# The first product of three token blocks as seven half-size products (Strassen), with its weight sums in the staging and attention memory

## The chip, the cores and the metric

The kernel runs on one core of a Trainium2 chip. A core has five engines that run side by side and meet only through semaphores: TensorE (PE in the profile; its weight loads are shown apart as PEld), VectorE (DVE), ScalarE (ACT), GpSimd (POOL) and SyncE (SP), which here issues nearly all DMAs. PE multiplies a stationary 128x128 tile with a moving tile of up to 512 columns and writes to PSUM, of which there are eight banks. The metric is the device time of one execution in microseconds, the median of several.

## The reference, cut to what matters

```python
kv = einsum('bhsd,bhse->bhde', k, v)                 # attention without softmax
o = einsum('bhsd,bhde->bhse', q, kv)
x = (o / sqrt(mean(o * o) + 1e-6) * g_norm)          # -> 2304 tokens x 512
h = x @ w_in                                         # first mixture: 512 -> 2048
g = h * tanh(softplus(h))
y = g @ w_out                                        # 2048 -> 512
h2 = y @ w2_in                                       # second mixture: 512 -> 1024
e = exp(h2 - max(h2)); s = h2 * e / sum(e)
ln = (s - mean(s)) / sqrt(var(s) + 1e-6) * g_ln
out = ln @ w2_out                                    # 1024 -> 512
```

Everything is in float32. The kernel holds each float32 operand of a product as two float16 halves, high and low, and makes three of the four products (high x high, high x low, low x high); so every product on PE costs three matmuls per 128 rows of contraction.

## The kernel before

The 2304 tokens are six blocks of 384 (`NB`, `BLK`). The first mixture goes by units (block, group): a group is four of the sixteen 128-wide slices of `w_in`'s output, so there are 24 units. A unit's first product is the task `H`: `h_mm` (line 636) makes, for each of four slices f, 12 matmuls of 128x384 (four slices of contraction, three passes) into one of three PSUM banks (`psH`, line of matmuls `hp<-xT,w`). ACT applies the activation straight from PSUM (`mish`, line 646, tile `m`), then writes the high half of g (`g_hi`, line 653), and DVE the low half (`g_lo`, line 658); three g buffers (`NG`) and three m buffers (`NM`) turn over. The second product is the task `Y`: `y_mm` (line 676), 48 matmuls of 128x384 per unit into four banks. Blocks 0 to 2 go in two halves of groups; blocks 3 to 5 (the late blocks) go through all four groups in turn, and their result is split to high and low by `y_hi` and `y_lo` (lines 704, 712).

Weights come as float32 pieces of 128x512 words: 16 of `w_in`, 16 of `w_out`, 8 of `w2_in`, 8 of `w2_out`, in the order of `PIECES`. Each is loaded into one of five staging slots (`st`), passes ACT, POOL and DVE to get an exact float32 (`w_scale`, `w_sign`, `w_low`, `w_put`, lines 542 to 559; tile `P`, five buffers), and is then split (`w_hi`, `w_lo`, lines 570, 577). The pieces of `w2_out` also get the factor `g_ln` (line 593) and the sums that a Strassen product needs (`w4_sums`, line 600), then their halves (lines 611, 615). Before the change `w2_in` has a tile of its own (`w3`) in memory that attention leaves when the last transposed x is there (`open_w34`), and `w2_out`'s sums are laid over `w_in`'s memory (`w4`), slice by slice as the last unit's products leave it.

The second mixture goes by 18 tiles of 128 tokens: `emit_H2` (line 753, 24 matmuls of 128x512), then a chain of maximum (DVE, line 764), exponential (ACT, 770), product with the sum (DVE, 779), variance (ACT, 786), norm (DVE, 814), and its split and transposing DMAs (lines 830, 836, 842). H2 of tile t waits for line 779 of tile t-2, which frees its PSUM banks. The output product of two tiles together, task `O` (`emit_O`, line 861), is already made as seven half-size products of 12 matmuls of 128x256, with the orders of `PROD` and `ORDER`, and combined through `o_keep`, `o_add` and `o_copy`.

The order of every engine's instructions is written by a planner. Every piece of work is a task with an engine, an estimated cost, its predecessors and sometimes a due time; `Plan.order` runs a list schedule over estimated times, and `Plan.search` repeats it 300 times with due times of early tasks moved at random and keeps the order whose estimated last PE task ends first. Each engine then gets its instructions in that order and works through them strictly in turn. Where the planned time of a PE task lies more than half a microsecond after the one before it, and before 150 us, `keep_warm` puts in matmuls on the identity (line 1200, 128x256) whose result nobody reads; here they are called fillers. They are executed whether or not the wait they stand for comes.

Of the kernel before, what the change touches and what calls it, by code (L numbers as in the profile page):

```python
# [36 lines left out]
class Plan:  # L37
    def __init__(self):
        self.tasks = {}
        self.behind = {}  # L40

# [68 lines left out]
    def search(self, turns, spread):  # L110
# [9 lines left out]
        for at, k in best:  # L120
            if self.tasks[k][5] is not None:
                self.tasks[k][5] = at
# [18 lines left out]
def tile_attn_moe_moe2(  # L141
# [57 lines left out]
    dec_p = ctx.enter_context(pool("dec", NDEC, side="right"))  # L199
# [19 lines left out]
    units += [(b, g) for b in range(NI, NB) for g in range(4)]  # L219
    line = ["H", "H", "H"]  # L220
# [11 lines left out]
    for u in pe:  # L232
        nominal[u] = at_
        at_ += 48 * MM if u[0] in "HY" else 24 * 0.216 if u[0] == "2" else 84 * 0.1095
# [244 lines left out]
    def a_xT(b, r):  # L479
        t = xhl_t.pop((b, r))  # L480
        if r == 0:
            if b == 2:
# [26 lines left out]
    def w3_item(j):  # L509
# [6 lines left out]
        return load, (lambda: (w34["w3"][:, c, 0, s], w34["w3"][:, c, 1, s])), None, 1  # L516
# [10 lines left out]
    PIECES += [("3", j) for j in range(8)] + [("4", j + o) for j in range(4) for o in (0, 4)]  # L527
# [3 lines left out]

    def w_load(u):
        t = st_all[:, PIECES.index(u) % NST]
        items[u][0](t)
        piece[u] = [t, None]

    def w_scale(u):

        piece[u][1] = dec_p.tile([128, 512], FP32, tag="P", name="P")
# [33 lines left out]
    def w_lo(u):  # L573
# [4 lines left out]
        else:  # L578
# [63 lines left out]

    def mish(b, grp, i):
# [6 lines left out]
    def g_hi(b, grp, i):  # L650
        if i == 0:
# [67 lines left out]
    def open_w34():  # L719
# [3 lines left out]
        w34["w3"] = p.tile([128, C, 2, F2], FP16, name="w3")  # L723
# [14 lines left out]
    T = {}  # L738

# [4 lines left out]
    def emit_H2(t):  # L744
        hp = ph2[t % 2].tile([128, 2, 512], FP32, tag="h2", name="h2")
        w3 = w34["w3"]
# [21 lines left out]
    def s_exp(t):  # L768
        e = T[t, "e"] = ph2["p"].tile([128, F2], FP32, tag="e", name="e", bufs=1)
# [83 lines left out]
    def emit_O(p, i):  # L853
# [5 lines left out]
        for kk in range(4):  # L859
            for la, wa in PASS:  # L860
                nc.tensor.matmul(  # L861
                    out=T[p, bank][:, 0:HB], lhsT=lnTs[p % 2][:, 8 * x + 4 * la + kk],
                    rhs=w4[:, kk, wa, w], start=(first and m == 0),
# [10 lines left out]
    def osb(p, t):  # L874
        if (p, "osb", t) not in T:
            T[p, "osb", t] = dec_p.tile([128, DM], FP32, tag="P", name="osb")
# [27 lines left out]
    load_after = {}  # L904

    for n, u in enumerate(PIECES):
        opened = ("open",) if u[0] in "34" else None
        if n < NST:
            before = []
        else:  # L910
            before = [("put", PIECES[n - NST])]
# [359 lines left out]
```

## Time and profile before

| | |
|---|---|
| median of 3 runs | 617.48 us (616.27 to 617.89) |
| the profiled execution | 616.5 us, its span 614.5 us |
| PE busy | 602.5 us (98%) |
| DVE, ACT, POOL busy | 365.0, 289.5, 95.9 us |
| granted TensorE clock | 1.0 in every slice (the upper level, 2.4 GHz) |
| HBM | 72 GB/s over the span |

The span runs from the first to the last instruction; the profiled time has 2.0 us around it. PE is busy from slice 1 to slice 40 with hardly a gap, so a time of this kernel is a sum over what PE has to issue, plus the few places where it waits. The other engines have idle time in every stage, but unevenly: DVE is at two to five tenths in the middle of the span and at eight to nine tenths in the first tenth and in most of the last third.

### The profile page before, as it was taken

The page shows a single profiled execution, that of the slowest core. Times are in us where ns is not written, and L with a number is a line of the kernel's source. Part 1 is how long each engine was busy: PE and PEld are TensorE (multiplying, and loading weights), DVE is VectorE, ACT ScalarE, POOL GpSimd, SP SyncE. Part 2 cuts the span into 40 slices and gives each one's busy share as a digit, 9 for nine tenths or more (in the row PEclk, how much of TensorE's full clock was granted, in tenths as well). Part 3 has the DMA queues.
Part 4 walks back from the last instruction along what each step waited for, and adds up shares of the span by engine and source line. Part 5 has one row for each costly group of instructions (what it writes and reads, how often), then busy time and mean ns, then how long its engine had stood idle before and what let it go on. Part 6 is the DMA issues. An engine that isn't in the chain of part 4 may idle for free.

```text
span 614.5 us, 10823 instructions
## 1 busy us (share of the span) xinstructions
PE 602.5 (98%) x4427; PEld 382.7 (62%) x4427; DVE 365.0 (59%) x626; ACT 289.5 (47%) x498; POOL 95.9 (16%) x126
## 2 busy tenths in 40 slices
PE   7998999999999999999999999999999999999997
PEld 6676666666666665666666656664445756675586
DVE  1788788882023541334212258995978678878881
ACT  3668557663323423333333266763545535454551
POOL 1534532310000210012101133210011000000000
PEclk9999999999999999999999999999999999999999
DMA  8999675842022250005100175300230993657466
GB/s 290 323 267 223 176 165 172 264 102 73 1 78 71 59 129 1 0 18 77 28 1 2 24 259 197 104 0 2 50 71 1 178 226 95 138 102 149 92 144 149
DMA packets 125904, 69.11 MB, mean 112 GB/s; under 512 B 100000, under 2 KB 117408, under 8 KB 125856
## 3 DMA queue, kind: packets, MB, share of 16 engines
q1 hardware_dynamic: 125696, 68.44, 45.7%
q8 instruction: 34, 0.56, 0.4%
q14 instruction: 14, 0.11, 0.1%
q10 hardware_dynamic: 160, 0.00, 0.0%
HBM read 39.33 MB, written 4.72 MB: 72 GB/s over the span
## 4 chain that ended last, share of the span: by engine, by line
PE 90%; DMA 6%; ACT 2%; issue 1%; DVE 1%; POOL 0%; SPq 0%; POOLq 0%; ACTq 0%
PE y L676 31%; PE hp L636 29%; PE h L753 15%; PE op L861 12%; DMA st<-in_moe_w_in_dram 3%; PE kvp L297 2%; PE xo L435 1%; DMA w<-g 1%; DMA qraw<-in_q_dram 1%; DMA xT<-xhl 1%; DMA yT<-in_k_dram 1%; ACT P L542 0%; POOL rho L457 0%; PE rT L373 0%; ACT m L646 0%
## 5 line engine op out<-in xcount | busy, mean ns | idle before, releaser
L676 PE MATMUL y<-g,w 128*128 128x384 f16 x1152 | 201.2, 326 | 0.0
L636 PE MATMUL hp<-xT,w 128*128 128x384 f16 x960 | 166.0, 326 | 0.6 <-DMA xT<-xhl 0.6
L636 PEld LDWEIGHTS <-w 128*128 128x128 f16 x1152 | 111.9, 98 | 74.3 <-issue 1.2
L676 PEld LDWEIGHTS <-w 128*128 128x128 f16 x1152 | 111.8, 98 | 73.9
L658 DVE SCALAR_TENSOR_TENSOR g<-m,g 128x768 f16<-128x768 f32 x48 | 46.2, 963 | 85.8 <-ACT g L653 85.8
L646 ACT ACTIVATE m<-hp 128x384 f32<-128x384 f32 x96 | 46.3, 488 | 107.6 <-PE hp L636 106.9
L753 PE MATMUL h<-w,yT 128*128 128x512 f16 x432 | 96.0, 379 | 0.0
L861 PE MATMUL op<-w,w 128*128 128x256 f16 x756 | 85.2, 273 | 1.8 <-DMA w<-g 1.0
L861 PEld LDWEIGHTS <-w 128*128 128x128 f16 x756 | 73.8, 98 | 13.5 <-DMA w<-g 1.3
L753 PEld LDWEIGHTS <-yT 128*128 128x128 f16 x432 | 42.3, 98 | 48.0
L547 POOL TENSOR_SCALAR st<-st 128x512 f32<-128x512 f32 x48 | 42.9, 903 | 110.6 <-ACT P L542 110.6
L653 ACT ACTIVATE g<-m 128x768 f16<-128x768 f32 x48 | 40.2, 839 | 13.2 <-PE y L676 12.6
L552 DVE SCALAR_TENSOR_TENSOR st<-st 128x512 int32<-128x512 int32 x48 | 35.9, 759 | 12.0 <-POOL st L547 12.0
L542 ACT ACTIVATE P<-st 128x512 f32<-128x512 f32 x48 | 32.0, 673 | 19.3 <-DMA st<-in_moe_w_in_dram 12.2
L455 POOL TENSOR_SCALAR ms<-ms 128x8 f32<-128x8 f32 x15 | 5.4, 363 | 210.5 <-DVE ms L450 210.1
L559 DVE SCALAR_TENSOR_TENSOR P<-P,st 128x512 int32<-128x512 int32 x48 | 34.9, 748 | 0.1
L636 PE MATMUL hp<-yT,w 128*128 128x384 f16 x192 | 33.3, 326 | 0.0
L805 POOL TENSOR_SCALAR var<-var 128x1 f32<-128x1 f32 x18 | 4.3, 241 | 168.4 <-DVE var L800 168.4
L786 ACT ACTIVATE e<-Q,nmz 128x1024 f32<-128x1024 f32 x18 | 20.7, 1148 | 20.6 <-DVE nmz L782 20.5
L764 DVE TENSOR_REDUCE mx<-h 128x1 f32<-128x1024 f32 x18 | 22.0, 1221 | 11.9 <-PE h L753 11.9
L770 ACT ACTIVATE e<-h,nb 128x1024 f32<-128x1024 f32 x18 | 20.0, 1110 | 15.7 <-DVE nb L765 8.5
L779 DVE SCALAR_TENSOR_TENSOR Q<-h,e 128x1024 f32<-128x1024 f32 x18 | 21.9, 1219 | 6.5 <-ACT e L770 6.5
(105 smaller groups left out, 518.5 us busy)
## 6 DMA issues: line engine op xcount, KB each, us to landing
st<-in_moe_w_in_dram SPq DMA_DIRECT2D x24, 512.0 KB, 5.7
st<-in_moe_w_out_dram SPq DMA_DIRECT2D x24, 512.0 KB, 4.1
yT<-in_k_dram SPq DMA_DIRECT2D x16, 288.0 KB, 5.3
yT<-in_v_dram SPq DMA_DIRECT2D x16, 288.0 KB, 5.6
out_dram<-osb SPq DMA_DIRECT2D x18, 256.0 KB, 2.8
qraw<-in_q_dram SPq DMA_DIRECT2D x3, 768.0 KB, 6.1
qraw<-in_q_dram SPq DMA_DIRECT2D x4, 384.0 KB, 8.3
qraw<-in_q_dram SPq DMA_DIRECT2D x4, 192.0 KB, 5.0
```

The costliest lines, as they stand in the source:

```text
L542: nc.scalar.activation(out=P, in_=v[:, :, 1], func=ACTF.Copy, scale=2.0 ** -111)
L547: nc.gpsimd.tensor_scalar(out=v[:, :, 1], in0=v[:, :, 1], scalar1=0.0, scalar2=1.0, op0=ALU.mult, op1=ALU.mult)
L552: nc.vector.scalar_tensor_tensor(out=v[:, :, 0], in0=v[:, :, 0], scalar=29, in1=v[:, :, 1], op0=ALU.logical_shift_right, op1=ALU.bitwise_or)
L559: nc.vector.scalar_tensor_tensor(out=P.bitcast(I32), in0=P.bitcast(I32), scalar=3, in1=v[:, :, 0], op0=ALU.logical_shift_left, op1=ALU.bit ...
L636: nc.tensor.matmul(out=h_t[b, grp, i], lhsT=w1[:, f, c, wa], rhs=xT_t[b][:, C * xa + c], start=(c == 0 and m == 0), stop=(c == C - 1 and m ...
L646: nc.scalar.activation(out=m_t[b, grp, i // 2][:, i % 2], in_=h_t.pop((b, grp, i)), func=ACTF.Mish, scale=2.0 ** -16)
L653: nc.scalar.activation(out=g_t[b, grp][:, 0, 2 * i:2 * i + 2], in_=m_t[b, grp, i], func=ACTF.Copy, scale=64.0)
L658: nc.vector.scalar_tensor_tensor(out=g_t[b, grp][:, 1, j], in0=m_t.pop((b, grp, i)), scalar=64.0, in1=g_t[b, grp][:, 0, j], op0=ALU.mult, ...
L676: nc.tensor.matmul(out=y_t[cc][:, 0:BLK], lhsT=w2[:, grp * G + ii, wa, cc * 128:(cc + 1) * 128], rhs=g_t[b, grp][:, ga, ii], start=(first ...
L753: nc.tensor.matmul(out=hp[:, half], lhsT=y[:, c, ya, tok], rhs=w3[:, c, wa, half * 512:(half + 1) * 512], start=(m == 0), stop=(m == 3 * C ...
L764: nc.vector.reduce_max(out=mx, in_=T[t, "hp"], axis=AX.X)
L861: nc.tensor.matmul(out=T[p, bank][:, 0:HB], lhsT=lnTs[p % 2][:, 8 * x + 4 * la + kk], rhs=w4[:, kk, wa, w], start=(first and m == 0), stop ...
```

## The change

The first product of blocks 3 to 5 is made as a 2x2 by 2x2 block product in seven block products. The unit (512 contraction rows x 512 outputs x 384 tokens) is cut in half in each of the three; a block product `h_prod` is 12 matmuls of 128x192 (two output slices, two slices of contraction, three passes). Per unit these are 84 matmuls of 128x192 where there were 48 of 128x384. Three of the products use the plain weights and three the plain x, the others sums of them:

- `conv_w` makes the four sums of a group's weights from its halves, in float32 on DVE, and splits the sums again (ACT and DVE): once for each of four groups. `conv_x` does the same for x of each late block. They go one after the other through one scratch `W_` of 2048 words, which is staging slots 2 and 3.
- The sums `ws` lie in staging slots 0 and 1 (group 0), in the `P` buffers (group 1), and in a tile that is opened where attention lay (groups 2 and 3). The sums of x lie in `yT[3]`, `yT[4]` and one more `xT` buffer.
- The seven products go into the three `psH` banks in the order 1, 2, 6, 7, 5, 4, 3; products 6, 5, 4 and 3 add on top of a bank after it was copied out: `h_keep` (ACT) copies a bank, `h_add` (DVE) adds a bank to a copy, `h_act` (ACT) applies the activation, twice from memory and once from PSUM.

What had its place there moves: `w2_in`'s halves are now laid over `w_in` groups 0 and 1, so their last two steps wait for the last block's products of these groups; the pieces of both `w2` matrices pass four staging slots and four `P` buffers, the first two slots being free only after the last block's group 0, the other two after the last sums; `w2_out`'s sums lie in four places and are made in the order 2, 3, 0, 1; the exponential's output shares memory with the scratch of `w4_sums`, so the first exponential waits for the last split of `w2_out`. The transposes of x for the late blocks get fixed due times (190, 222 and 246 us). Since the tasks changed, the planner's search ends in another order everywhere, the first 60 us included.

```diff
 PIECES += [("1", f) for f in range(8, 16)] + [("2", f) for f in range(8, 16)]
-    PIECES += [("3", j) for j in range(8)] + [("4", j + o) for j in range(4) for o in (0, 4)]
+    PIECES += [("3", j) for j in range(8)] + [("4", j + o) for j in (2, 3, 0, 1) for o in (0, 4)]
...
+    w3 = w1f[:, 0:2 * C * F2].rearrange("p (c a n) -> p c a n", c=C, a=2)
...
+    ws = {0: st_w[:, 0:2048].bitcast(FP16), 1: dec_w[:, 0:4096]}
...
+    W_ = st_w[:, 2048:4096].bitcast(FP32)
+    he = st_w[:, 4096:5120].bitcast(FP32)
...
+    def conv_w(g, step):
+        V = W_.rearrange("p (f c n) -> p f c n", f=G, c=C)
+        if step < 2:
+            f = slice(G * g + 2 * step, G * g + 2 * step + 2)
+            nc.vector.tensor_tensor(
+                out=V[:, 2 * step:2 * step + 2].rearrange("p f c n -> p (f c) n"),
+                in0=w1[:, f, :, 0].rearrange("p f c n -> p (f c) n"),
+                in1=w1[:, f, :, 1].rearrange("p f c n -> p (f c) n"), op=ALU.add)
+        elif step < 6:
+            o, x, y, op = c_sums(w_view(V))[step - 2]
+            nc.vector.tensor_tensor(out=o, in0=x, in1=y, op=op)
+        else:
...
+            if not lo:
+                nc.scalar.activation(out=d[:, 0, s], in_=W_[:, s], func=ACTF.Copy)
+            else:
+                nc.vector.tensor_tensor(
+                    out=d[:, 1, s], in0=W_[:, s], in1=d[:, 0, s], op=ALU.subtract)
...
+    HPROD = {1: (0, 0, 0, 0, 0, 0, "A", True), 2: (0, 0, 1, 0, 1, 0, "B", True),
+             6: (1, 0, 0, 1, 1, 1, "A", False), 7: (1, 1, 0, 1, 0, 1, "D", True),
+             5: (1, 1, 1, 1, 0, 0, "A", False), 4: (0, 1, 1, 1, 1, 0, "D", False),
+             3: (1, 0, 1, 0, 1, 1, "A", False)}
...
+    def h_prod(b, grp, i):
+        ww, m, k, xx, kx, n, bank, opens = HPROD[i]
+        p = h_bank(b, grp, bank)
+        S = ws[grp].rearrange("p (a f c n) -> p a f c n", a=2, f=G, c=C)
+        x = xs[b] if xx else xT_t[b]
+        for fs in range(2):
+            f = 2 * m + fs
+            for c in range(2):
+                for j, (wa, xa) in enumerate(PASS):
+                    lhsT = S[:, wa, f, 2 * k + c] if ww else w1[:, G * grp + f, 2 * k + c, wa]
+                    nc.tensor.matmul(
+                        out=p[:, HT * fs:HT * fs + HT], lhsT=lhsT,
+                        rhs=x[:, C * xa + 2 * kx + c, HT * n:HT * n + HT],
...
+    def h_keep(b, grp, n):
+        p = h_bank(b, grp, {1: "A", 2: "A", 7: "D"}[n])
+        nc.scalar.activation(out=h_e(b, grp, n), in_=p[:, 0:BLK], func=ACTF.Copy)
...
+    def h_add(b, grp, m, n, bank, e):
+        p = h_bank(b, grp, bank)
+        nc.vector.tensor_tensor(
+            out=h_m(b, grp, m)[:, :, HT * n:HT * n + HT],
+            in0=p[:, 0:BLK].rearrange("p (f t) -> p f t", f=2),
+            in1=h_e(b, grp, e).rearrange("p (f t) -> p f t", f=2), op=ALU.add)
...
+        elif n < 36:
+            before = [("put", v) for v in PIECES[27:32]]
+            before += [("H", NB - 1, 0, 0)] if n < 34 else [("cx", NB - 1, 9), ("cw", 3, 9)]
         else:
-            before = [("put", PIECES[n - NST])]
+            before = [("put", PIECES[n - 4])]
...
         task(("whi", u), "A", 0.71 if scaled else 0.62, w_hi, (u,),
-             [("put", u), ("gs",) if u[0] == "1" else None])
+             [("put", u), ("gs",) if u[0] == "1" else None,
+              ("H", NB - 1, u[1] // 4, 0) if u[0] == "3" else None])
...
+    convs = [("cw", 0), ("cw", 1), ("cx", 3), ("cw", 2), ("cw", 3), ("cx", 4), ("cx", 5)]
...
+            needs += {6: [("he", b, grp, 1)], 5: [("he", b, grp, 2)], 4: [("he", b, grp, 7)],
+                      3: [("hc", b, grp, 22)]}.get(i, [])
+            task(("Hp", b, grp, i), "P", 12 * 0.0826, h_prod, (b, grp, i), needs, 0.25,
+                 T0 + 0.99 * j)
...
         task(("ex", t), "A", 1.3, s_exp, (t,),
-             [("mx", t)] + ([("sq2", t - 1)] if t else []))
+             [("mx", t)] + ([("sq2", t - 1)] if t else [("w4lt", 1)]))
```

How the order moves is shown at three places. The first is PE in the first 60 us, around the fillers (line 1200 before, 1447 now), where PE waits for pieces of `w_in` and the transposed q and x of block 1 (`xo` is attention's product). Before:

```order
L636 MATMUL hp<-xT,w_68 128x384
L1200 LDWEIGHTS ident
L1200 MATMUL hp<-ident 128x256
...
L1200 MATMUL hp<-ident 128x256
L435 LDWEIGHTS qT
L435 MATMUL xo<-kvr_94,qT 128x128
...
L1200 LDWEIGHTS ident
L1200 MATMUL hp<-ident 128x256
...
L1200 MATMUL hp<-ident 128x256
L636 LDWEIGHTS w_68
L636 MATMUL hp<-xT,w_68 128x384
```

Now:

```order
L1447 LDWEIGHTS ident
L1447 MATMUL hp<-ident 128x256
...
L1447 MATMUL hp<-ident 128x256
L658 LDWEIGHTS w_68
L658 MATMUL hp<-xT,w_68 128x384
...
L1447 LDWEIGHTS ident
L1447 MATMUL hp<-ident 128x256
...
L658 LDWEIGHTS w_68
L658 MATMUL hp<-xT,w_68 128x384
```

Before there were fillers in runs of 29, 19 and 9, with one tile of attention's product between the first two; now there are runs of 8, 25, 36 and 15, each followed by one slice (12 matmuls) of the first product. The first five fillers of the first mixture and the 13 ahead of it are the same in both.

The second place is ACT in the late blocks, where the first pieces of `w2_in` are scaled (tile `P`, line 542 before, 553 now). Before, between activations of block 5 (`m<-hp`), with `w_3657` the tile of `w2_in`:

```order
L646 ACTIVATE m<-hp 128x384
L542 ACTIVATE P<-st 128x512
L570 ACTIVATE w_3657<-P 128x512
L646 ACTIVATE m<-hp 128x384
L542 ACTIVATE P<-st 128x512
L653 ACTIVATE g<-m 128x768
```

Now, between the copies of units (4, 0) and (4, 1) (`st<-hp` and `e<-hp`):

```order
L770 ACTIVATE e_3519<-hp 128x384
L553 ACTIVATE P<-st 128x512
L792 ACTIVATE m<-m 128x768
L804 ACTIVATE g<-m 128x768
L553 ACTIVATE P<-st 128x512
L792 ACTIVATE m<-hp 128x2x192
L804 ACTIVATE g<-m 128x768
L770 ACTIVATE st<-hp 128x384 x2
```

Two scalings now stand ahead of the last steps of unit (4, 0) and of the copies that products 6 and 5 of unit (4, 1) wait for.

The third is DVE where the second mixture begins (`mx` is the maximum of its first tile, `t` the scratch of `w4_sums`, `w_68` the memory of `w_in`). Before:

```order
L615 TENSOR_TENSOR w_68<-P,w_68 128x256
L615 TENSOR_TENSOR w_68<-P,w_68 128x512
L615 TENSOR_TENSOR w_68<-t_3658,w_68 128x1024
L764 TENSOR_REDUCE mx<-h_4262 128x1
L765 TENSOR_SCALAR nb<-mx 128x1
L779 SCALAR_TENSOR_TENSOR Q,sz<-h_4262,e 128x1024
```

Now:

```order
L918 TENSOR_REDUCE mx<-h_4788 128x1
L919 TENSOR_SCALAR nb<-mx 128x1
L636 TENSOR_TENSOR w_68<-t_2996,w_68 128x1024
L636 TENSOR_TENSOR w_68<-P,w_68 128x256
L636 TENSOR_TENSOR w_68<-P,w_68 128x512
L933 SCALAR_TENSOR_TENSOR Q,sz<-h_4788,t_2996 128x1024
```

The last splits of `w2_out` now stand behind the first maximum instead of ahead of it, and the tile `t` that they read is the one that the first exponential writes.

## Rows read from the trace of the kernel before

**Rows 1.** The page: busy time, share of the span and count.
```profile
PE 602.5 (98%) x4427; PEld 382.7 (62%) x4427; DVE 365.0 (59%) x626; ACT 289.5 (47%) x498; POOL 95.9 (16%) x126
```
**Rows 2.** The page: chain that ended last, by line.
```profile
PE y L676 31%; PE hp L636 29%; PE h L753 15%; PE op L861 12%; DMA st<-in_moe_w_in_dram 3%; PE kvp L297 2%; PE xo L435 1%; DMA w<-g 1%; DMA qraw<-in_q_dram 1%; DMA xT<-xhl 1%; DMA yT<-in_k_dram 1%; ACT P L542 0%; POOL rho L457 0%; PE rT L373 0%; ACT m L646 0%
```
**Rows 3.** Waits of PE, whole span: total us, times, longest.
```profile
PE xo L435 <- DMA qT<-qhl: 1.7, 1, 1.7
...
PE op L861 <- DMA w<-g: 1.0, 1, 1.0
PE op L861 <- DVE osb L880: 0.8, 2, 0.4
PE hp L636 <- DMA xT<-xhl: 0.6, 1, 0.6
```
**Rows 4.** Groups by shape, line 636: shapes, count, busy us, mean ns, idle before.
```profile
L636 PE MATMUL hp<-xT,w 128*128 128x384 f16 x960 | 166.0, 326 | 0.6 <-DMA xT<-xhl 0.6
L636 PEld LDWEIGHTS <-w 128*128 128x128 f16 x1152 | 111.9, 98 | 74.3 <-issue 1.2
```
**Rows 5.** Timeline of PE at 62 to 69 us: start, duration, count.
```profile
62.20 6.01 PE L636 MATMUL hp<-xT,w 128*128 128x384 f16 x36
68.05 0.83 PE L435 MATMUL xo<-kvr,qT 128*128 128x128 f16 x12
68.72 2.11 PE L636 MATMUL hp<-xT,w 128*128 128x384 f16 x12
```
**Rows 6.** Timeline of PE at 575 to 578 us.
```profile
575.05 2.78 PE L861 MATMUL op<-w,w 128*128 128x256 f16 x24
577.67 5.34 PE L753 MATMUL h<-w,yT 128*128 128x512 f16 x24
```
**Rows 7.** Timeline of the weight loads at 50 us.
```profile
49.89 0.67 PEld L435 LDWEIGHTS <-qT 128*128 128x128 f16 x12 [1.98 <-DMA qT<-qhl]
```
**Rows 8.** Timeline of PE at 44 to 61 us, the fillers.
```profile
44.86 3.33 PE L1200 MATMUL hp<-ident 128*128 128x256 f16 x29
...
50.57 2.24 PE L1200 MATMUL hp<-ident 128*128 128x256 f16 x19
...
54.59 1.15 PE L1200 MATMUL hp<-ident 128*128 128x256 f16 x9
...
60.26 2.11 PE L676 MATMUL y<-g,w 128*128 128x384 f16 x12
```
**Rows 9.** Groups by shape on ACT and DVE.
```profile
L653 ACT ACTIVATE g<-m 128x768 f16<-128x768 f32 x48 | 40.2, 839 | 13.2 <-PE y L676 12.6
...
L696 DVE SCALAR_TENSOR_TENSOR yf<-y,yT 128x384 f32<-128x384 f32 x12 | 6.6, 554 | 17.7 <-PE y L676 17.5
...
L615 DVE TENSOR_TENSOR w<-t,w 128x1024 f16<-128x1024 f32 x4 | 4.9, 1219 | 0.2 <-ACT w L611 0.2
```
**Rows 10.** Timeline at 390 to 392 us, all engines: from PE's end to ACT's copy.
```profile
389.92 2.11 PE L676 MATMUL y<-g,w 128*128 128x384 f16 x12
...
392.07 0.49 ACT L704 ACTIVATE yT<-y 128x384 f16<-128x384 f32 x1 [0.64 <-PE y L676]
```
**Rows 11.** Stretches: us, then busy us of PE, PEld, DVE, ACT, POOL, clock, DMA.
```profile
228.00:355.00 127.00, 127.00 (x889) 77.59 (x885) 34.73 (x48) 40.78 (x70) 11.00 (x12) 1.00 0.13 24
355.00:415.40 60.40, 60.40 (x373) 36.38 (x372) 50.37 (x76) 40.77 (x71) 14.97 (x16) 1.00 0.39 136
```
**Rows 12.** Timeline at 352 to 358 us: first load of `w2_in`, first use.
```profile
352.90 2.82 SPq L514 DMA_DIRECT2D st<-in_moe_w_in_dram  x5
...
357.73 0.67 ACT L542 ACTIVATE P<-st 128x512 f32<-128x512 f32 x1 [0.27 <-DMA st<-in_moe_w_in_dram]
```
**Rows 13.** Timeline of DVE at 417 to 426 us.
```profile
417.17 1.23 DVE L615 TENSOR_TENSOR w<-t,w 128x1024 f16<-128x1024 f32 x1 [0.18 <-ACT w L611]
420.65 1.23 DVE L764 TENSOR_REDUCE mx<-h 128x1 f32<-128x1024 f32 x1 [2.25 <-PE h L753]
...
424.95 1.22 DVE L779 SCALAR_TENSOR_TENSOR Q<-h,e 128x1024 f32<-128x1024 f32 x1 [2.89 <-ACT e L770]
```
**Rows 14.** Chain of waits: H2 of tiles 0 and 1, then of tile 2.
```profile
415.43 10.36 PE h L753 x48
...
427.74 5.18 PE h L753 x24
```

More of the change, by code (lines that the diff above doesn't have):

```diff
@@ L120, in search @@
         for at, k in best:
-            if self.tasks[k][5] is not None:
+            if self.tasks[k][5] is not None and k not in self.hints:
                 self.tasks[k][5] = at
@@ L219, in tile_attn_moe_moe2 @@
     units += [(b, g) for b in range(NI, NB) for g in range(4)]
+    sevens = [u for u in units if u[0] >= NI]
     line = ["H", "H", "H"]
@@ new lines, in conv_x @@
+    def conv_x(b, step):
+        X = W_[:, 0:C * BLK].rearrange("p (c t) -> p c t", c=C)
+        if step < 2:
+            c = slice(2 * step, 2 * step + 2)
+            nc.vector.tensor_tensor(
+                out=X[:, c], in0=xT_t[b][:, c], in1=xT_t[b][:, C + 2 * step:C + 2 * step + 2],
+                op=ALU.add)
+        elif step < 6:
+            v = [X[:, 2 * k:2 * k + 2, HT * n:HT * n + HT] for k in range(2) for n in range(2)]
+            o, x, y, op = x_sums(v)[step - 2]
+            nc.vector.tensor_tensor(out=o, in0=x, in1=y, op=op)
+        else:
+            lo, h = divmod(step - 6, 2)
+            if b not in xs:
+                xs[b] = yT[b].rearrange("p c a t -> p (c a) t") if b < NB - 1 else xt_p.tile(
+                    [128, 2 * C, BLK], FP16, tag="xT", name="xs")
+            c = slice(2 * h, 2 * h + 2)
+            d = slice(C + 2 * h, C + 2 * h + 2)
+            if not lo:
+                nc.scalar.activation(out=xs[b][:, c], in_=X[:, c], func=ACTF.Copy)
+            else:
+                nc.vector.tensor_tensor(
+                    out=xs[b][:, d], in0=X[:, c], in1=xs[b][:, c], op=ALU.subtract)
@@ L722, in open_w34 @@
         p = w34_cm[0].__enter__()
-        w34["w3"] = p.tile([128, C, 2, F2], FP16, name="w3")
+        x = p.tile([128, 2 * 4096], FP16, name="ws")
+        for i in range(2):
+            ws[i + 2] = x[:, 4096 * i:4096 * i + 4096]
+        w4[3] = seven(x[:, 0:14 * HB])
+        part_e[0] = x[:, 16 * HB:24 * HB].bitcast(FP32).rearrange("p (e n) -> p e n", e=4)
+        w34["P"] = p.tile([128, 3, 512], FP32, name="P")
+        w34["osb"] = x[:, 24 * HB:32 * HB].bitcast(FP32).rearrange("p (n c) -> p n c", n=2)
         w34["t4"] = p.tile([128, 4, 256], FP32, name="t4")
@@ L862, in emit_O @@
                     out=T[p, bank][:, 0:HB], lhsT=lnTs[p % 2][:, 8 * x + 4 * la + kk],
-                    rhs=w4[:, kk, wa, w], start=(first and m == 0),
+                    rhs=w4[kk][:, wa, w], start=(first and m == 0),
                     stop=(m == 11), skip_group_check=not first,
@@ L1225, in tile_attn_moe_moe2 @@
     task(("zero",), "G", 2.0, setup, (1,))
+    for key, due in ((("xT", 3, 2), 190.0), (("xT", 4, 2), 222.0), (("xT", 5, 2), 246.0)):
+        plan.tasks[key][5] = due
+        plan.hints.add(key)
     order = plan.search(300, 8.0)
```

189 lines of the change are left out of this document (164 added, 25 removed).

## The prediction

> **What bounds the kernel now.** I read the page's engine line first: PE is busy 98% of the span and no other engine over 60% [rows 1]. The reader should ask next whether that is one chain or a mean over stages, and the chain of waits answers it: its steps are PE's own lines, `Y` 31%, `H` 29%, H2 15%, `O` 12% [rows 2]. The waits of PE, taken by engine, then show how little it stands still behind the head: 1.7 us for a transposed q and 0.6 us for a transposed x in the first 60 us, 1.0 and 0.8 us in the output products [rows 3]; before `H` it waited 0.6 us over all of its matmuls [rows 4]. So a change in what PE has to issue reaches the end nearly one to one, as long as no new wait appears; and the few waits that exist are small change that a new order can win or lose.
>
> **The products.** Durations of pipelined matmuls overlap (326 ns is the mean of one [rows 4]), so I take start-to-start times. Thirty-six matmuls of 384 columns fill 62.20 to 68.05: 162.5 ns each. Twelve of 128 columns fill 68.05 to 68.72: 55.8 ns [rows 5]. Twenty-four of 256 columns fill 575.05 to 577.67: 109.2 ns [rows 6]. The steps are equal (53.3 ns per 128 columns), so 192 columns, which no row shows, should take the middle of 55.8 and 109.2: 82.5 ns. Removed are 12 units x 48 = 576 matmuls x 162.5 ns = 93.6 us; added 12 x 84 = 1008 x 82.5 ns = 83.2 us. Gain 10.4 us, all on the path.
>
> Each matmul has its own weight load, and there are 432 more. A load lasts 98 ns [rows 4], more than 82.5. But twelve loads of the 128-column products took 0.67 us together [rows 7], 56 ns apart: loads overlap one another, so I take no cost for them. Bounds: 55.8 ns (hidden even at 128 columns) and 98 ns (one load after the other).
>
> The Trainium skill speaks against this at one place: "TensorE: Matmul & The Clock Gate", section "Back-to-back issue gap", gives about 81 ns for a sustained pair of load and matmul at 128 columns and 131 ns at 512. By it 192 columns would lie near 89 ns and the gain be 3.6 us instead of 10.4. The trace has 55.8 ns where the page says 81, and 216 ns (10.36 us for 48 [rows 14]) where it says 131, so here the measurement decides against it.
>
> **The fillers.** The new order has 84 fillers in the first 60 us after the first five, the old one 57: 27 more x 109.2 ns = 2.95 us of PE. Net of products and fillers: -7.5 us.
>
> **Waits in the first 60 us.** Before, PE lost 57 x 109 ns = 6.2 us to these fillers [rows 8] and 1.7 + 0.6 us to real waits: 8.5 us. The 84 fillers alone are 9.2 us, so if weights and transposes come as before, the old waits are covered. Nothing in the trace shows the new order of loads, so from -2.3 (none left) to +2.0 (the old ones and as much again beside the new fillers). I take -1.3, nearer to none.
>
> **Sums of weights and x.** Per group of weights 4 instructions of 1024 columns at 1.22 us and 4 of half that: 7.4 us of DVE; per block of x three quarters of it, 5.5 us; 4 x 7.4 + 3 x 5.5 = 46 us. The 36 `h_add` at 0.55 us add 20 us [rows 9]. ACT gets two splits of 1.05 us per group and 1.6 us per block (13 us), and per unit three copies and three activations where four activations were (+1.4 us, 16 us in all). In the order the sums of groups 0, 1 and of block 3 stand well ahead of unit (3, 0); the rest, some 30 us, falls where DVE was busy 34.7 of 127 us and ACT 40.8 [rows 11]. Cost nothing: PE's matmuls hide them. If that cover went, products 6 and 7 of units (3, 2), (3, 3), (4, 0) would be late next.
>
> **Copies between products.** Products 6, 5, 4 wait for a copy by ACT, product 3 for an `h_add`, each with one product (0.99 us) as cover where no part of `Y` stands between. A part of `Y` that started at 389.92 was done at 392.03, 0.16 us after its last issue, and ACT began 0.04 us later and took 0.49 [rows 10]: 0.69 us, margin 0.3. The `h_add`: 0.75, margin 0.24. So on free engines PE does not wait. A `g_hi` (0.84 us [rows 9]) just begun makes a copy late by up to 0.54. In ACT's order the copies mostly stand ahead of the two `g_hi`. I take +0.8 us (two or three such hits), bounds 0 and 5 (half of the 36 copies that have no `Y` for cover late by 0.3).
>
> **The second mixture's weights.** The loads of `w2_in` now start after the last sums of x; behind them SP has only `w2_out`'s loads, but ACT's first two scalings stand ahead of the copies for unit (4, 1). From issue to use took 4.8 us before [rows 12]. By the order, the last sums end about 10 us of PE ahead of product 6 of (4, 1); 4.8 us of load, two scalings (1.35), two activations and two `g_hi` (3.0) and a copy (0.5) make 9.7. It just fits; included in the +0.8.
> The rest starts when block 5 has left group 0. From there PE has 21 products (20.8 us) and 17 parts of `Y` (33.2): 54 us to H2, and 5.2 more to the first maximum. Before, DVE was busy 50.4 us of the 60.4 in which the same pieces were split [rows 11]; now two pieces are half done ahead (-3) and nine `h_add` come on top (+5): 52 of 59 us. Before, the last split ended at 418.4, three us into H2 [rows 13, 14]. Now three splits stand between first maximum and the product that frees H2's banks, of which only the first (1.22 us) holds up the exponential: line 779, over at 426.2 [rows 13], would end at 427.4, and tile 2 starts at 427.74 [rows 14]. Margin 0.3; what the split is later than planned goes to PE. I take +0.8, bounds 0 and 4 (the idle tenth of DVE lost).
>
> **Output products.** `O` of tiles 0 and 1 now begins after six H2 instead of seven, in runs of two to five products between H2s instead of twelve at once. The 1.0 and 0.8 us of [rows 3] came from the run of twelve, where pair 1's transposes were late, and from the end, where now 24 products instead of 21 follow the last H2. I take -1.4, bounds -1.8 and +2.
>
> **Sum.** -7.5 - 1.3 + 0.8 + 0.8 - 1.4 = -8.6 us. The profiled execution took 616.5 (span 614.5 and 2.0 around it): 607.9. The median of the runs is 1.0 above it: 609. With every small term at its better end 606, so 606 to 612.5 is the likeliest case's own range.
>
> **Rivals.**
> - *Weight loads set the pace* (slower). Place: the 1008 pairs of `h_prod`. Price at 98 ns: 98.8 us instead of 83.2, +15.6: 624.6. It decides from 91 ns per pair on, where the gain is gone. For it: 98 > 82.5 [rows 4]. Against: [rows 7]. The same section of the skill's page stands nearer to this than to me, and its "LDWEIGHTS (loading the stationary operand)" gives 107 ns for 128 columns; the trace has 98, overlapped. Chance 0.05.
> - *Copies at every unit* (no change). If each of the 36 copies costs 0.25 us, 9 us instead of 0.8: 617. For it: margins of 0.3 us behind engines that take turns. Against: `O` has the same scheme with 1.31 us of cover and waited 0.8 us over 63 products [rows 3]. Chance 0.07.
> - *Second weights late* (smaller gain). The loads take longer than 4.8 us or DVE loses its idle tenth: +4 to +6: 613 to 615. For it: margins of 0.3 us at two places. Against: ACT and POOL have room. Chance 0.12.
> - *Head later*. New waits beside the new fillers: +2.0 instead of -1.3: 612.5, and block 2's x, now behind more loads of `w_in`, could add 2. Chance 0.11.
>
> **Numbers.** My case has 0.65. A measurement of this kernel can't tell less than 0.3% (1.9 us) from no change, so faster means below 615.6. Faster: 0.65 + 0.11 + 0.09 of the late weights = 0.85; same: 0.05 of the copies and 0.03 of the late weights, 0.08; slower: the weight loads and 0.02 of the copies, 0.07. The range for 8 in 10 goes from 604.8 (all small terms good and one more us) to 615.8, the end of the late weights.
>
> **What would show it.** Right: a group `hp<-...` 128x192 x1008 whose runs of 12 start 0.99 us apart, PE busy near 595, no wait of PE above 1 us between 230 and 400, H2 of tile 0 starting near 411 (two parts of `Y`, 3.9 us, that stood behind its start now stand ahead). Weight loads: runs of 12 of 1.1 us or more. Copies: many short waits of PE for ACT `h_keep` or DVE `h_add`. Late weights: PE waiting for DVE line 933 of tile 0, or H2 for the split of `w2_in`. Head: `H` waiting for a DMA or for `w_lo` before 110 us, and `Y` beginning after 61. Wrong altogether: idle PE in a stage I have not named, above all between 60 and 230, where the order changed only because the search ended elsewhere.

## The result and the profile after

The changed kernel takes 607.25 us (median of 4 runs, 605.34 to 609.9) against 616.96 us before (4 runs, 616.27 to 617.89): ratio 0.9845, 95% interval 0.9802 to 0.9887. Run again beside the experiments it took 606.82 us (4 runs) against 617.18 (9 runs), ratio 0.9838, interval 0.9817 to 0.9859. So it is 9.7 to 10.4 us faster. Its first profiled execution, the one read here, took 608.13 us with a span of 606.1.

The page's engine line (busy us, share of the span, count) answers to [rows 1], the chain by line to [rows 2]:

```profile
PE 595.8 (98%) x4886; PEld 412.2 (68%) x4886; DVE 424.6 (70%) x718; ACT 316.5 (52%) x536; POOL 94.9 (16%) x126
...
PE y L827 27%; PE h L907 15%; PE hp L753 14%; PE op L1015 14%; PE hp L658 11%; DMA yT<-in_v_dram 2%; PE kvp L300 2%; DMA st<-in_moe_w_in_dram 2%; DMA qraw<-in_q_dram 2%; PE xo L438 1%; DVE st L563 1%; DVE P L570 1%; DMA yT<-xhl 1%; POOL rho L460 1%; SPq L274 1%
```

PE has 6.7 us less to do and is again the chain's engine. The sums, copies and additions show in full on the helpers, 60 us more on DVE and 27 on ACT, and none of their lines is in that list of the chain. The plain `H` of blocks 0 to 2 is now line 658, the seven products line 753, `Y` 827, H2 907, `O` 1015.

The waits of PE over the whole span (total us, times, longest), as in [rows 3]:

```profile
PE kvp L300 <- DMA yT<-in_v_dram: 2.6, 2, 1.9
PE idle L1447 <- POOL ident L1461: 1.3, 1, 1.3
PE xo L438 <- DMA qT<-qhl: 0.7, 1, 0.7
PE hp L658 <- ACT w L581: 0.6, 1, 0.6
PE hp L658 <- DMA xT<-xhl: 0.5, 1, 0.5
PE hp L658 <- DMA yT<-xhl: 0.5, 1, 0.5
PE qTp L331 <- DMA qraw<-in_q_dram: 0.3, 1, 0.3
PE hp L658 <- DVE w L590: 0.3, 1, 0.3
```

No line of the seven products, the second mixture or the output products is in this list: after 107 us PE waits nowhere, and the two waits of `O` in [rows 3] are gone. The stretches say the same (us, then busy us and count of PE, PEld, DVE, ACT, POOL, granted clock, DMA share, GB/s); lines 4 and 5 answer to [rows 11]:

```profile
0.00:30.00 30.00, 25.70 (x358) 19.05 (x360) 11.72 (x30) 15.27 (x32) 11.06 (x16) 1.00 0.97 305
30.00:62.00 32.00, 29.85 (x339) 21.22 (x336) 25.86 (x40) 21.97 (x40) 13.31 (x15) 1.00 0.88 206
62.00:107.00 45.00, 44.54 (x299) 27.42 (x297) 35.53 (x53) 27.09 (x48) 14.98 (x16) 1.00 0.69 175
...
228.00:355.00 127.00, 127.00 (x1168) 100.59 (x1164) 69.03 (x101) 57.75 (x97) 9.25 (x10) 1.00 0.13 30
355.00:415.40 60.40, 60.40 (x518) 45.85 (x517) 48.98 (x78) 42.34 (x72) 11.79 (x14) 1.00 0.33 106
415.40:480.00 64.60, 64.60 (x357) 34.82 (x356) 57.38 (x118) 35.61 (x53) 5.81 (x12) 1.00 0.34 61
480.00:603.00 123.00, 122.68 (x907) 88.44 (x904) 92.00 (x186) 55.88 (x91) 10.02 (x24) 1.00 0.72 139
```

DVE doubled between 228 and 355 us (34.7 to 69.0) under a PE that is busy throughout. The pace of a unit is in the chain of waits at 280 to 300 us (start, us, what):

```profile
285.49 1.95 PE y L827 x12
287.44 6.93 PE hp L753 x84
294.37 1.95 PE y L827 x12
296.32 0.99 PE hp L753 x12
```

84 matmuls of 192 columns, one whole unit with no `Y` in between, take 6.93 us: 82.5 ns each, and 12 take 0.99.

The head is where time was lost. The timeline of PE from 44 us, as in [rows 8] (start, us, line, count; in brackets what a wait was for):

```profile
44.24 1.05 PE L1447 MATMUL hp<-ident 128*128 128x256 f16 x8
45.12 2.11 PE L658 MATMUL hp<-xT,w 128*128 128x384 f16 x12
47.07 2.89 PE L1447 MATMUL hp<-ident 128*128 128x256 f16 x25
49.80 2.11 PE L658 MATMUL hp<-xT,w 128*128 128x384 f16 x12
51.75 4.09 PE L1447 MATMUL hp<-ident 128*128 128x256 f16 x36
56.45 0.50 PE L658 MATMUL hp<-xT,w 128*128 128x384 f16 x2 [0.61 <-ACT w L581]
57.24 1.80 PE L658 MATMUL hp<-xT,w 128*128 128x384 f16 x10 [0.29 <-DVE w L590]
58.88 1.80 PE L1447 MATMUL hp<-ident 128*128 128x256 f16 x15
61.22 2.11 PE L658 MATMUL hp<-xT,w 128*128 128x384 f16 x12 [0.54 <-DMA xT<-xhl]
63.17 2.11 PE L827 MATMUL y<-g,w 128*128 128x384 f16 x12
```

The longest run of fillers, 36, and the run of 15 each end in a real wait: what they stand for comes later than planned. `Y` begins at 63.17 instead of 60.26.

### The profile page after: what moved, and what is told of

Its sections match the earlier page's. It is cut to its first block, busy times and chain, and to the rows that moved or that the text cites. A ratio compares the mean times of both kernels' runs of the same rounds, so it can differ in the third digit from the quotient of the medians.

```text
span 606.1 us, 11871 instructions
## 1 busy us (share of the span) xinstructions
PE 595.8 (98%) x4886; PEld 412.2 (68%) x4886; DVE 424.6 (70%) x718; ACT 316.5 (52%) x536; POOL 94.9 (16%) x126
## 4 chain that ended last, share of the span: by engine, by line
PE 84%; DMA 7%; DVE 3%; POOL 1%; SPq 1%; ACT 1%; issue 1%; ACTq 0%; POOLq 0%
PE y L827 27%; PE h L907 15%; PE hp L753 14%; PE op L1015 14%; PE hp L658 11%; DMA yT<-in_v_dram 2%; PE kvp L300 2%; DMA st<-in_moe_w_in_dram 2%; DMA qraw<-in_q_dram 2%; PE xo L438 1%; DVE st L563 1%; DVE P L570 1%; DMA yT<-xhl 1%; POOL rho L460 1%; SPq L274 1%
## 5 line engine op out<-in xcount | busy, mean ns | idle before, releaser
L827 PEld LDWEIGHTS <-w 128*128 128x128 f16 x1152 | 110.9, 98 | 67.8
L658 PEld LDWEIGHTS <-w 128*128 128x128 f16 x576 | 55.5, 98 | 39.4 <-issue 2.0
L1015 PEld LDWEIGHTS <-w 128*128 128x128 f16 x756 | 74.0, 98 | 11.2
L558 POOL TENSOR_SCALAR st<-st 128x512 f32<-128x512 f32 x48 | 39.2, 822 | 224.0 <-ACT P L553 163.5
L658 PE MATMUL hp<-xT,w 128*128 128x384 f16 x384 | 66.6, 326 | 1.4 <-ACT w L581 0.6
L1015 PE MATMUL op<-w,w 128*128 128x256 f16 x378 | 51.5, 273 | 0.0
L797 ACT ACTIVATE m<-hp 128x384 f32<-128x384 f32 x48 | 23.1, 485 | 31.2 <-PE hp L658 30.4
L563 DVE SCALAR_TENSOR_TENSOR st<-st 128x512 int32<-128x512 int32 x48 | 34.3, 732 | 6.4 <-POOL st L558 6.3
L753 PEld LDWEIGHTS <-w 128*128 128x128 f16 x432 | 36.5, 98 | 2.7
L1015 PE MATMUL op<-P,w 128*128 128x256 f16 x189 | 30.9, 273 | 0.0
L1015 PE MATMUL op<-ws,w 128*128 128x256 f16 x189 | 30.9, 273 | 0.0
L792 ACT ACTIVATE m<-m 128x384 f32<-128x384 f32 (+1 forms) x24 | 16.3, 681 | 26.1 <-DVE m L779 25.9
L940 ACT ACTIVATE t<-Q,nmz 128x1024 f32<-128x1024 f32 x18 | 20.7, 1151 | 17.3 <-DVE nmz L936 17.1
```

The costliest lines, as they stand in the source:

```text
L558: nc.gpsimd.tensor_scalar(out=v[:, :, 1], in0=v[:, :, 1], scalar1=0.0, scalar2=1.0, op0=ALU.mult, op1=ALU.mult)
L563: nc.vector.scalar_tensor_tensor(out=v[:, :, 0], in0=v[:, :, 0], scalar=29, in1=v[:, :, 1], op0=ALU.logical_shift_right, op1=ALU.bitwise_or)
L658: nc.tensor.matmul(out=h_t[b, grp, i], lhsT=w1[:, f, c, wa], rhs=xT_t[b][:, C * xa + c], start=(c == 0 and m == 0), stop=(c == C - 1 and m ...
L753: nc.tensor.matmul(out=p[:, HT * fs:HT * fs + HT], lhsT=lhsT, rhs=x[:, C * xa + 2 * kx + c, HT * n:HT * n + HT], start=(opens and fs == 0 ...
L797: nc.scalar.activation(out=m_t[b, grp, i // 2][:, i % 2], in_=h_t.pop((b, grp, i)), func=ACTF.Mish, scale=2.0 ** -16)
L827: nc.tensor.matmul(out=y_t[cc][:, 0:BLK], lhsT=w2[:, grp * G + ii, wa, cc * 128:(cc + 1) * 128], rhs=g_t[b, grp][:, ga, ii], start=(first ...
```

## The experiments

The ratios are to the kernel before, with their 95% intervals. A difference from the changed kernel is the difference of the ratios (0.9838 for the changed kernel) times 617 us; each is uncertain by some 1.7 to 2.5 us, so that small ones are read from the traces.

### The changed kernel again

> The changed kernel again, on the chip of the runs beside it, so that they have a base. Theory: 607.3 us as before, 8 to 10 us below the kernel before; a ratio of 0.984. Rival (that the first comparison was luck of the chip): a ratio above 0.99.

606.82 us, ratio 0.9838. Its trace is the base below: span 606.0, last PE instruction over at 602.51. From the first seven-product matmul (236.69) to H2 (412.84) it needs 176.15 us, as in the first trace. In that stretch stand 1008 x 82.5 ns = 83.16, 47 parts of `Y` x 1.95 = 91.65 and two runs of attention x 0.67 = 1.34: 176.15. Nothing is left over for a wait.

### No fillers in the front stage

```
-            elif gap > 0.5 and at_time < 150 and done.issuperset(h_free[h_line[0]]):
-                keep_warm(int((gap - 0.2) / 0.12), h_open(h_line[0]))
```

> The changed kernel without the 93 filler matmuls inside the first mixture's front stage (those before the stage stay). The theory that fillers stand in front of waits that are there anyway: the waits take their place, the clock stays granted, and the time moves by less than 1.5 us. Rival A, fillers cost their whole length: 93 x 109.2 ns = 10.2 us, so about 597 us. Rival B, the fillers keep the clock: stretches at a granted clock below 1.0 appear in the first 70 us, and the time rises by several us.

606.91 us, ratio 0.984 (0.9818 to 0.9862): no difference. (By the trace they are 89, 9.7 us.) The timeline of PE shows what took their place:

```profile
47.18 0.50 PE L658 MATMUL hp<-xT,w 128*128 128x384 f16 x2 [1.68 <-ACT w L581]
48.58 1.80 PE L658 MATMUL hp<-xT,w 128*128 128x384 f16 x10 [0.90 <-DVE w L590]
54.59 3.87 PE L658 MATMUL hp<-xT,w 128*128 128x384 f16 x12 [4.20 <-ACT w L581]
59.27 2.11 PE L658 MATMUL hp<-xT,w 128*128 128x384 f16 x12 [0.81 <-DMA xT<-xhl]
```

Twelve matmuls of 384 columns take 3.87 us after the wait of 4.20 and 2.11 otherwise, and the stretch's granted clock (the third column from the right) falls:

```profile
56.00:60.00 4.00, 3.19 (x14) 1.55 (x13) 3.46 (x5) 2.15 (x4) 1.01 (x1) 0.75 0.73 173
```

PE's idle time up to 107 us rises from 6.27 to 13.40 us (+7.1), the matmuls behind the wait lose 1.8, the fillers' 9.7 us go: -0.8, and the last PE instruction ends 0.9 us earlier (601.59). Theory right in its sum, but not in the clock, which it had staying granted; there Rival B is right, at a smaller price: fillers hide waits that are there anyway, and what they cost beyond that is nearly what the clock would cost.

### Seven products for two blocks

```
-    sevens = [u for u in units if u[0] >= NI]
+    sevens = [u for u in units if u[0] > NI]
```

(The planner's nominal cost of a unit follows the same condition.)

> Seven products only for the blocks 4 and 5; block 3 is multiplied as in the kernel before. Theory (the gain lies in the columns that TensorE streams): four units go back from 84 x 82.5 ns to 48 x 162.5 ns, 4 x 0.87 = +3.5 us against the changed kernel, if the head's order costs the same; the head is planned anew, and its waits may move by some 2 us either way, so 608.7 to 612.7. Rival (the gain comes from the new order of the head and not from the products): no more than 1 us, or a change by more than 6 us.

608.38 us, ratio 0.9861 (0.984 to 0.9882): +1.4. The size lies below the expected range, and with an uncertainty of 1.8 us the time alone doesn't exclude the rival's 1 us. The trace ends at 602.53, as the base does; four units cost 3.5 us more by the pitches, and the head, which the planner wrote anew, shows 13.4 us of idle time and fillers up to 107 us (3.8 and 88 x 0.109) where the base has 17.4 (6.27 and 102 x 0.109). So by this count the dose is there and the head gave as much back.

### Half the columns per matmul

```
+                    for q in range(2):
+                        at_q = HT // 2 * q
                         nc.tensor.matmul(
-                            out=p[:, HT * fs:HT * fs + HT], lhsT=lhsT,
+                            out=p[:, HT * fs + at_q:HT * fs + at_q + HT // 2], lhsT=lhsT,
...
```

> Each matmul of 192 columns is issued as two of 96 columns with the same weights: 2016 instead of 1008 weight loads in the seven-product units, the same columns streamed. Theory (a load of the weights lies beneath the stream, and the pace is the columns'): if 96 columns still hide a load, 2016 x 41 ns against 1008 x 82.5 ns, within 1 us of the changed kernel; if a load takes no less than the 56 ns that matmuls of 128 columns show, 2016 x 56 - 1008 x 82.5 = +29.7 us, about 637. Rival (already at 192 columns the loads set the pace, 82.5 ns is a load's own length): 2016 x 82.5 ns, +83 us.

610.11 us, ratio 0.9897 (0.9871 to 0.9923): +3.6. The chain of waits, one unit:

```profile
286.85 7.14 PE hp L755 x168
```

7.14 / 168 = 42.5 ns. From the first seven-product matmul to H2 it is 178.67 us, 2.52 more than the base: 1008 added matmuls x 2.5 ns. Theory right in kind, with the columns' pace and not the loads'; its "within 1 us" left out the 2.5 ns that each added matmul brings. The rival is out. But the same weights came two or four times in a row, which the next kernel makes rarer.

### Half the columns, other weights each time

```
+            for q in range(2):
+                at_q = HT // 2 * q
                 for c in range(2):
                     for j, (wa, xa) in enumerate(PASS):
...
```

> As the halves, but TensorE first runs the left 96 columns of all six matmuls of a sum and then the right 96 columns, so that no two matmuls in a row have the same weights: 2016 loads of which each brings other weights. With the same weights twice in a row a matmul of 96 columns took 42.5 ns (168 in 7.14 us). Theory (a load of other weights lies beneath 96 columns as well): 42.5 ns again, 609 to 611 us. Rival (a load of other weights takes TensorE longer than that, at most the 55.8 ns of a matmul of 128 columns, and the repeated weights had saved it): 2016 x 55.8 - 1008 x 82.5 ns = +29 us, 636.

610.75 us, ratio 0.9911 (0.9877 to 0.9945): +4.5. The chain of waits, one unit:

```profile
287.21 7.14 PE hp L755 x168
```

The same 42.5 ns, the same 178.67 us from the first matmul to H2. The edit does not quite do what I expected of it: `PASS` uses the high half of the weights in two passes running, so two of three loads bring other weights, not every one (with the halves before it was one of three). The trace settles it even so: at each of the six places of a sum the next matmul starts 42 or 43 ns later, whether its weights are the same or others. A load of other weights, 98 ns long in the records, lies beneath even 96 columns.

### Copies twice

```
-        nc.scalar.activation(out=h_e(b, grp, n), in_=p[:, 0:BLK], func=ACTF.Copy)
+        for _ in range(2):
+            nc.scalar.activation(out=h_e(b, grp, n), in_=p[:, 0:BLK], func=ACTF.Copy)
```

> Each of the 36 copies of a product out of its bank is issued twice on ScalarE (36 x 0.49 us more, order of all engines the same). In the trace of the changed kernel a copy ends some 0.48 us before TensorE opens the bank again, where a single product (0.99 us) stands between, in two or three places of each of the 12 units; elsewhere output products stand between. Theory (the copies have just that margin, less 0.25 us of handing over): 0.2 to 0.3 us of waiting at 24 to 30 places, +5 to +8 us. Rival A (the banks don't bind, the copies are free): within 1 us. Rival B (each copy stands on TensorE's path): 36 x 0.49 = +17.6 us.

610.31 us, ratio 0.9894 (0.9877 to 0.991): +3.5. From the first seven-product matmul (234.86) to H2 (414.57) it is 179.71 us, 3.56 more than the base, or 0.10 us for each of the 36 copies. The chain of waits at one unit (start, us, what):

```profile
285.45 1.99 PE hp L753 x24
287.44 0.02 issue
287.46 0.50 ACT st L771
287.96 0.02 issue
287.99 0.49 ACT st L771
...
289.84 3.13 PE hp L753 x36
```

Theory right in kind, its size too high: the copies enter the chain at once when they are twice as long, but at 12 places (by 0.27 to 0.47 us from start to start) instead of the 24 to 30 that I counted. Both rivals are out. One thing for the reader: the list of waits names only 0.6 us here, and PE's idle time in the stretch is 1.64 us, against 3.56 us of delay. A matmul of 192 columns is recorded as 246 ns and the next starts 82.5 ns later, so a wait below some 0.16 us disappears in the record of the one before it. Delays that small are seen only from start to start.

### The last split five times

```
-            nc.vector.tensor_tensor(
-                out=w4[j][:, 1, q], in0=x, in1=w4[j][:, 0, q], op=ALU.subtract)
+            for _ in range(5 if (j, which) == (1, "t") else 1):
+                nc.vector.tensor_tensor(
+                    out=w4[j][:, 1, q], in0=x, in1=w4[j][:, 0, q], op=ALU.subtract)
```

> The last low part of w2_out (1.21 us on VectorE, just ahead of the first exponential of the second mixture) is computed five times in place of once: +4.9 us on VectorE at the handover. Theory (the third tile of the second mixture's first product stands 0.66 us behind what it needs, and nothing gives the time back later): TensorE waits 4.9 - 0.66 = 4.2 us there and the time rises by 4 us, to 611. Rival (the handover has several us to spare, as the absence of any wait there suggests): no wait, within 1 us.

613.21 us, ratio 0.9941 (0.992 to 0.9961): +6.4. The timeline of PE at the handover:

```profile
417.78 5.34 PE L908 MATMUL h<-w,yT 128*128 128x512 f16 x24
422.96 2.11 PE L828 MATMUL y<-g,w 128*128 128x384 f16 x12
429.56 6.87 PE L908 MATMUL h<-w,yT 128*128 128x512 f16 x24 [4.49 <-DVE Q L934]
```

and the stretches around it:

```profile
425.00:429.50 4.50, 0.07 (x1) 0.00 (x0) 2.81 (x5) 2.49 (x3) 0.00 (x0) 0.97 0.00 0
429.50:432.60 3.10, 3.04 (x8) 1.11 (x9) 2.18 (x9) 2.45 (x4) 0.75 (x2) 0.50 0.00 0
```

The wait is the forecast one, on the forecast line: five splits took 6.25 us instead of 1.21, and 4.49 us of the 5.04 reached PE, so the changed kernel has 0.55 us to spare there. The rest is the clock: after 4.5 us without a matmul the granted clock is 0.50, the lower of its two levels, for 3 us, and the 24 matmuls need 6.71 us from start to start instead of 5.18, 1.5 more. 4.5 + 1.5 = 6.0, and the last PE instruction ends 5.95 us after the base's. The rival is out.

### Other orders of the same work

In each of five kernels only the planner's random numbers (and in the first the length of its search) differ:

```
-        rng = random.Random(1)
+        rng = random.Random(6)
...
-    order = plan.search(300, 8.0)
+    order = plan.search(2500, 8.0)
```

> The changed kernel with the planner's search run from other random numbers and 2500 turns long in place of 300; it moves instructions in the first 160 us alone. Theory (the head's waits and fillers, some 15 us of the first 107, are a matter of the order found): 1 to 3 us come off, 604 to 606, with fewer fillers and the rest of the trace the same. Rival (the head is bound by its loads, 0.92 of the DMA engines' time to 62 us, so no order helps): within 0.6 us of 607.

> The kernel before, its planner's search of 300 turns run from other random numbers (the second set). The head took some 2.5 us more from the change than forecast; this run and the three beside it (the kernel before and the changed one, each in two other orders) ask whether that is a price of the change or the luck of the order found. Theory (luck: before stands in a good order, the changed kernel in a middling one): before in other orders is 1 to 2 us slower than before, 618 to 619, with more waiting and fillers in its first 107 us. Rival (the change makes the head longer, orders matter little): within 0.7 us of before.

> The kernel before in an order from the fourth set of random numbers. Theory (luck of the order): 1 to 2 us slower than before, 618 to 619. Rival (a price of the change): within 0.7 us of before.

> The changed kernel in an order from the sixth set of random numbers, 300 turns. Theory (luck of the order): 1 us or more faster than the changed kernel, 604.5 to 606. Rival (a price of the change): within 0.7 us of 607.

> The changed kernel in an order from the eleventh set of random numbers, 300 turns. Theory (luck of the order): 1 us or more faster than the changed kernel, 604.5 to 606. Rival (a price of the change): within 0.7 us of 607.

The column of idle time and fillers is PE's, up to 107 us, from one trace each (idle plus fillers x 0.109 us). Each ratio is to the kernel before as it ran beside it (616.7 to 617.2 us).

| order | us | ratio | 95% | idle + fillers |
|---|---|---|---|---|
| before, as it is | 617.18 | 1 | | 6.7 + 8.2 = 14.9 |
| before, second numbers | 619.24 | 1.0041 | 1.0026 to 1.0056 | 5.9 + 10.3 = 16.1 |
| before, fourth numbers | 616.61 | 0.999 | 0.9977 to 1.0002 | 5.2 + 10.4 = 15.6 |
| changed, as it is | 606.82 | 0.9838 | 0.9817 to 0.9859 | 6.3 + 11.1 = 17.4 |
| changed, sixth numbers, long | 606.95 | 0.9837 | 0.9817 to 0.9857 | 4.4 + 9.7 = 14.1 |
| changed, sixth numbers | 607.36 | 0.985 | 0.983 to 0.9869 | 7.6 + 10.7 = 18.3 |
| changed, eleventh numbers | 608.49 | 0.986 | 0.9838 to 0.9882 | 6.3 + 10.3 = 16.5 |

My theory of luck fell in four of the five runs: only one order of before is slower as I said, and no order of the changed kernel is faster. The rival's figures come in three of the five (the long search, the fourth numbers, the sixth), so it fits better, but an order can move the time by some 2 us: the second numbers do. The clock has a part in that, which the table's last column leaves out: at 25.46 us of that trace twelve matmuls of 128 columns (line 373) take 1.54 us, and 0.88 elsewhere. The stretch around them (the granted clock is the third figure from the right) has no wait above 0.4 us:

```profile
25.00:30.00 5.00, 4.54 (x87) 3.83 (x87) 2.97 (x6) 4.00 (x8) 0.41 (x1) 0.74 1.07 378
```

Over three orders before the mean is 617.7, over four of the changed kernel 607.4: the gain is 10.3 us, about what it is for the pair as it is. In these single traces the head's idle time and fillers go from 14.9 to 16.1 us before and from 14.1 to 18.3 after, so whether the change itself makes the head longer stays open. The long search's trace ends at 599.97, 2.5 us before the base's, but it is the fastest of its four runs and their median is no better. No kernel here beats the changed one.

## Why the prediction was right, step by step

The forecast was 609.0 with faster as the likeliest, and the median is 607.25. The last PE instruction ends at 602.68 us instead of 611.07: -8.4 us, where the sum said -8.6. The terms:

- **Products, -10.4: right.** 82.5 ns was interpolated from the pitches of [rows 5, 6], and one unit of 84 takes 6.93 us. All of it is on the path.
- **Weight loads, nothing: right, and further than claimed.** I argued from loads 56 ns apart [rows 7]; the two kernels of half the columns ran at 42.5 ns with twice the loads, so the rival of the loads never had a place. The Trainium skill ("TensorE: Matmul & The Clock Gate", "Back-to-back issue gap") gives about 81 ns for a load and a matmul of 128 columns; pairs of 96 columns at 42.5 ns don't agree with that, and the measurement decides. The spacing that the same section gives for a single matmul at full clock, the columns at 2.4 GHz and 2.5 ns, is what the streams here keep at 96, 192 and 384 columns.
- **Fillers, +2.95: right as a count.** 102 of them in all against 75, and PE is busy with them. What they cost is another thing: leaving 89 out changed the time by nothing, since waits and a slower clock took their place. A filler is no cost of its own where what it stands for is late.
- **Sums of weights and x, nothing: right.** DVE has 60 us more where I had 66, ACT 27 where I had 29, and PE waits for none of it.
- **Waits in the first 60 us, -1.3: wrong, this is the step that failed.** I let the new fillers cover the old waits, and I counted 2.3 us of these. The same view has others, of which I passed over these two (v from HBM, and `xf`, the x of attention before it is split):

```profile
PE kvp L297 <- DMA yT<-in_v_dram: 1.4, 1, 1.4
PE hp L1200 <- DVE xf L384: 1.3, 1, 1.3
```

  PE's idle time up to 107 us went from 6.73 us (4.41 and 2.32 in the stretches up to 30 and to 62 us) to 6.91 (4.30, 2.15 and 0.46): +0.2. In the second trace of the same kernel it is 6.27, so -0.5, still short of -1.3. The wait for q [rows 3] shrank from 1.7 to 0.7 us and the one for `xf` is gone, but the one for v grew by 1.2, one of 0.5 for a transposed x came at 106.8 us, and two new ones for the split of `w_in` (0.6 and 0.3; the first is not in the second trace) stand right behind the run of 36 fillers. A filler covers a wait only as far as the planner had foreseen it.
- **Copies and additions between products, +0.8: nothing.** The stretch from the first of the seven products to H2 is 176.15 us, exactly the sum of its matmuls. The margin of 0.3 us was read about right, for a third of the copies: made twice, 0.49 us longer, they cost 3.56 us at 12 places. The hits of a `g_hi` on a copy that I priced did not reach PE.
- **The second mixture's weights, +0.8: nothing.** H2 of tile 0 started at 413.01, not near 411, because the head was later; the two parts of `Y` do stand ahead of it as I had them (89 parts instead of 87). Tile 2 started without a wait. The timeline of PE before, then now (its last row is cut off by the end of the view), and then that of DVE, as in [rows 13]:

```profile
415.27 10.52 PE L753 MATMUL h<-w,yT 128*128 128x512 f16 x48
```

```profile
413.01 10.52 PE L907 MATMUL h<-w,yT 128*128 128x512 f16 x48
423.37 2.11 PE L827 MATMUL y<-g,w 128*128 128x384 f16 x12
425.32 4.91 PE L907 MATMUL h<-w,yT 128*128 128x512 f16 x22
```

```profile
418.45 1.22 DVE L918 TENSOR_REDUCE mx<-h 128x1 f32<-128x1024 f32 x1
...
419.77 1.21 DVE L636 TENSOR_TENSOR w<-t,w 128x1024 f16<-128x1024 f32 x1
420.90 1.02 DVE L636 TENSOR_TENSOR w<-P,w 128x256 f16<-128x256 f32 x2
423.59 1.22 DVE L933 SCALAR_TENSOR_TENSOR Q<-h,t 128x1024 f32<-128x1024 f32 x1 [1.67 <-ACT t L924]
```

  Line 933 is over at 424.8, H2 of tile 2 begins at 425.32. The margin that I worked out as 0.3 is 0.55 by the split made five times. So the margin was as thin as I had it: one more split of 1.2 us would exceed it by some 0.7, though the 4 to 6 us of the rival take four or five.
- **Output products, -1.4: -1.8.** Both waits of [rows 3] are gone.

Products -10.4, fillers +2.95, idle time in the head +0.2, output products -1.8 make -9.1; 0.7 us is left over, the net of PE's busy time. It holds 0.45 from six fillers at 4.8 us, which took 1.28 us instead of 0.83. That is the execution and not the change (0.83 in the kernel with the copies twice, 1.46 in before with the second numbers), and PE waits for v behind them either way. The rest I can't assign to a line.

The start of H2 divides the whole better. It came 2.3 us earlier: 10.4 from the products, less 3.9 for the two parts of `Y` that now stand ahead of it, less 4.3 that the head took. For the head I had 2.95 - 1.3 = 1.65, so it was 2.6 us worse. By its own signs the rival *Head later* came about, with 2.6 of its 3.3 us: `H` waits for a DMA and for `w_lo` before 110 us, and `Y` begins at 63.17. Behind that start, without the two parts of `Y`, 2.2 us were gained, where copies, handover and output products together stood at +0.2: 2.4 us better. That these two cancel is luck, and no run separates what the change did to the head from what the order found did.

The sum is made for the profiled execution, and this took 608.13 us where it said 607.9. The median of the runs lies 0.9 us below it where I had put it 1.0 above; most of the distance between 609 and 607.25 is this.

## What to carry to other kernels

Where one engine is busy through whole stages, price a change to its instructions by the pitch from start to start of like rows, and interpolate between shapes. What is hung on the other engines then costs nothing until its margin is used up, so look for the margin and not for the busy share: here 27 and 60 us more were free, while 0.5 us more in each copy and 5 us more in one split reached PE at once. An order that a planner finds anew is a cost or gain of its own, here up to some 2 us, and should have its own term and range.

## What the runs showed of the hardware

- The pitch of matmuls with 96, 192 and 384 columns was 42.5, 82.5 and 162.5 ns, and 55.8 and 109.2 ns at 128 and 256: 2.5 ns and the columns at 2.4 GHz, with a weight load each, recorded at 98 ns. Halving 192 columns cost 2.5 ns a piece and no more.
- Waits of 4.2 and 4.5 us of PE were each followed by some 3 us at the lower clock level (24 matmuls of 512 columns in 6.71 us instead of 5.18, or twelve of 384 in 3.87 instead of 2.11), 1.5 to 1.8 us on top of the wait. The changed kernel's own waits, of 1.9 us and less, left the granted clock at 1.00 in every stretch up to the end of PE's work. But length alone doesn't decide: in the order of the long search the stretch from 15 to 20 us is at 0.66, with one wait of 0.52 us in it, behind twelve matmuls of two columns, and in the kernel before with the second numbers the stretch from 25 to 30 us is at 0.74, behind waits of 0.34 and 0.42 us.
- At the very start the stretches say 1.00 as well, but seven fillers of 256 columns took 1.68 us there, where 109 ns each would be 0.77. The pace tells the level in these first microseconds, not the row.
